# Weights decoded by a sign-carrying Prelu, and all exponentials added ahead of one round of sums

## The chip, the core and the metric

The kernel runs on one core of a Trainium2 chip. The metric is the device time of one execution in microseconds (us). The engines are TensorE (PE, its weight loads PEld), VectorE (DVE), ScalarE (ACT), GpSimd (POOL) and SyncE (SP, which issues every DMA here).

## The reference

Attention with a soft cap, then two feed-forward blocks, all in float32, 2 x 448 tokens, 12 heads of 64:

```python
scores = cap * np.tanh(scale * (q @ k.T) / cap)
attn = np.exp(scores - max); attn = attn / (attn.sum(-1) + 1e-09)
x = attn @ v                                   # 896 tokens x 768
h = x @ w_in                                   # 768 x 2048
g = (a0 + a1*h + a2*h**2 + a3*h**3) / (1 + |b0|*|h| + |b1|*h**2 + 1e-6)
x = g @ w_out                                  # 2048 x 768
h = max(x @ w1, x @ w2, x @ w3)                # three of 768 x 768
out = h @ moe2_w_out                           # 768 x 768
```

The weights come as 64-bit floats. The kernel reads each as two 32-bit words and makes a float32 of them on the chip.

## The kernel before

**Stages.** Heads are worked in six groups d0 to d5 of four heads each (two pairs r). For a group, `scores` (products at L616 and L624) makes seven score tiles; ACT takes tanh of each (L638, or L641 in halves) and then the exponential (L645), once over the three full key tiles of a pair and once over the shared rest of the keys. `weighted_rest` and `weighted` (L669, L688) multiply the exponentials with v. `summed` makes the sums of the exponentials: products with a matrix of ones (L734), four small ones for each tile. Where `ADDED[d]` is 2 (d0 to d2) the three full tiles of a pair are first added on DVE or POOL (`added`, L710), and the products run over that sum and the rest of the keys: 2 rounds. Where it is 0 (d3 to d5) they run over all four: 4 rounds. The sums go through a copy (L745), a DMA out and back, an addition of the guard and a reciprocal (L753, L754), and two more DMAs into a row tile; `scale_pair` multiplies (L776) and splits the result into a high and a low part (L780, L784), the x of the next stage.

Then `up` (L804) multiplies x with w_in in parts of six products, `up` and `rational` make g (L821 to L869), `parts` splits g (L883, L886), `down` multiplies with w_out (L911), `product` with w1 to w3 (L1048) and `output` with the last matrix (L1156). Each product with split operands is three TensorE products.

**Weights.** `decoded` makes a float32 tile of 128 x 768 from a raw tile (768 pairs of words, one DMA of 768 KB). `scale` multiplies the upper words by 2^-112, on ACT (L446) or POOL (L448); `shift` shifts by three and clears the sign (L452, DVE); `rest` puts in three low bits, on DVE (L471) or by a byte copy on ACT (L468); `sign` puts the sign back (L461, DVE). `split` rounds to a high part (L488) and takes the low part (L491).

**What sets the order.** A planner (`Flow`) lays out every operation with a cost, engines that it may run on and due times that follow from TensorE's order; each engine then runs its list in that order, and none overtakes. `SPARE`, `AHEAD`, `NEAR`, `SWITCH` and the costs in `add` are its figures, so a changed cost or operation reorders all engines.

Of the kernel before, what the change touches and what calls it, by code (L numbers as in the profile page):

```python
# [11 lines left out]
U8 = mybir.dt.uint8  # L12
# [16 lines left out]
QGUARD = 1.0 + 1e-6  # L29
CAP = 6  # L30
# [5 lines left out]
WARM = 3  # L36
EARLY = 5

AHEAD, NEAR, LEAVE = 200.0, 30.0, 4
# [7 lines left out]
SPARE = 1.06  # L47
# [11 lines left out]
ADDED = 2, 2, 2, 0, 0, 0  # L59
# [10 lines left out]
class Op:  # L70
    def __init__(self, engines, after, vals, fn, shared, due, leave, ahead, size, mode):
        self.engines, self.after, self.vals, self.fn = engines, after, vals, fn
        self.shared, self.due, self.leave, self.ahead, self.size = shared, due, leave, ahead, size
        self.mode = mode
        self.next, self.soft, self.left, self.ready, self.done, self.on = [], [], 0, 0.0, None, None
# [6 lines left out]
class Flow:  # L82
# [91 lines left out]
    def issue(self):  # L174
# [21 lines left out]
        while left:  # L196
# [4 lines left out]
            while moved:  # L201
                moved = False
                for e in names:
# [5 lines left out]
                    for op in ready:  # L209
# [23 lines left out]
                        if e != first and op.engines[e] > max(0.0, busy[first] - t) + ahead[first] + cost + (not self.scores and e == "act") * BIAS:  # L233
                            ahead[first] += cost
                            continue
# [83 lines left out]
def attention_moe(ctx: ExitStack, tc: tile.TileContext, qk, v, w_in, w_out, w123, w_out2, par, out):  # L319
# [22 lines left out]
    qone = cp.tile([P, 1], F32, name="qone")  # L342
    ones = cp.tile([P, 3, Q], F32, name="ones")
# [50 lines left out]
    con_in = dma(lambda: con, lambda: par.broadcast_to([P, 8]), size=0.004, issue=0.45, due=-20.0)  # L394
# [11 lines left out]
    def first_scalars(e):  # L406
        dve.reciprocal(out=qscale, in_=cap)
        dve.tensor_scalar(out=qscale, in0=qscale, scalar1=D**-0.5, scalar2=None, op0=ALU.mult)
        dve.memset(qone, QGUARD)

    def more_scalars(e):
# [5 lines left out]
    scal = add({"act": 0.8}, more_scalars, [con_in], due=60.0)  # L417
# [3 lines left out]
        [scal], due=60.0,  # L421
# [8 lines left out]
    add({"pe": 3 * WARM * 0.4}, warm_up, [zero], [idle, warm])  # L430
    fl.clock = 4.5
# [7 lines left out]
    def decoded(key, src):  # L439
# [39 lines left out]
        s1 = add({"act": 0.80, "pool": 0.87}, scale, [got], [raw, dec], leave=LEAVE, ahead=AHEAD)  # L479
        s2 = add({"dve": 0.47}, shift, [s1], [dec], shared=True)  # L480
        s3 = add({"dve": 0.87, "act": 1.9}, rest, [s2], [raw, dec], shared=True)
        s4 = add({"dve": 0.87}, sign, [s3], [raw, dec], shared=True)
# [90 lines left out]
    def prep(pi):  # L573
        raw = slot(f"qk{pi}")
        src = qk[divmod(pi, NPAIR)]
        QK[pi] = raw, dma(lambda: two(raw), lambda: src, vals=[raw], size=0.459, issue=0.45, ahead=NEAR)
# [18 lines left out]
    def scores(d, i):  # L595
# [22 lines left out]
        def ends(e):  # L618
# [11 lines left out]
            {"pe": FULL}, products if whole_ else ends, [QK[pi][1] for pi in pis], [QK[pi][0] for pi in pis] + [t],  # L630
# [73 lines left out]
    def added(d, r):  # L704
        y, done = slot(f"es{d}_{r}"), None
        for n in range(ADDED[d]):
# [5 lines left out]
            done = add({"dve": 1.0, "pool": 2.1}, plus, [ex, ez, done], [x, y, z], shared=True)  # L712
        ADDS[d, r] = y, done, lambda: two(y)

    def summed(d):
# [5 lines left out]
        for r in range(2):  # L721
# [3 lines left out]
            rounds.append(es + [E[d, 2 * NFULL]])  # L725
        last = len(rounds[0]) - 1

        def products(e):
            for n in range(last + 1):
                for r in range(2):  # L730
                    x = rounds[r][n][2]()
                    for j in range(2):
                        g = (2 * r + j) * Q
                        pe.matmul(  # L734
                            bank(t)[g : g + Q, :S], ones[:, 0 if n < last else 1 + r], x[:, j], start=n == 0,
# [8 lines left out]
        got = add(  # L744
            {"act": 0.43, "dve": 0.54}, lambda e: copy_on[e](rows[row.at[0]], bank(t)[:, :S]), [dep], [t, row]  # L745
        )
# [5 lines left out]
        def recip(e):  # L752
            dve.tensor_scalar(out=comp[d], in0=comp[d], scalar1=guard, scalar2=None, op0=ALU.add)  # L753
            dve.reciprocal(out=comp[d], in_=comp[d])  # L754

        rc = add({"dve": 0.75}, recip, [back, guard_in])
# [34 lines left out]
    def up(n):  # L791
# [28 lines left out]
        def absolute(e):  # L820
            act.activation(two(a_)[:, i], bank(h)[:, :S], AF.Abs)  # L821
# [4 lines left out]
        def linear(e):  # L826
            if e == "act":
                act.activation(two(t_)[:, i], two(a_)[:, i], AF.Identity, bias=b0, scale=b1)  # L828
            else:
                engine[e].tensor_scalar(  # L830
                    out=two(t_)[:, i], in0=two(a_)[:, i], scalar1=b1, scalar2=b0, op0=ALU.mult, op1=ALU.add
                )
# [398 lines left out]
```

## Time and profile before

| | us |
|---|---|
| median of 3 runs (lowest, highest) | 491.92 (491.77, 492.22) |
| the profiled execution, its own time | 492.5 |
| span of the profiled execution | 490.4 |
| TensorE busy in the span | 482.6 |
| DVE busy | 415.2 |
| ACT busy | 337.2 |
| POOL busy | 91.8 |

The profile has one execution. The span runs from the first to the last instruction; 2.1 us of the execution lie around it. Busy TensorE time counts a product from its issue, so that waits can hide in it. A tile name ends in a number in the order of the instructions and has none in the profile. A line of a timeline is: start, time from the first start to the last end, engine, line, operation, tiles, shape, count, and in brackets the idle time before it with its releaser.

### The profile page before, as it was taken

The numbers are of one execution on the slowest core, as the hardware profiler recorded it, in microseconds if no ns is written. First come the engines' busy times: TensorE is split into PE (matmuls) and PEld (weight loads), VectorE is DVE, ScalarE is ACT, GpSimd is POOL, SyncE is SP. The second block draws the span as 40 slices with busy tenths as digits, with TensorE's granted clock in tenths as the row PEclk, the third lists the DMA queues.
The fourth block names the chain that finished last, engine by engine and source line by source line (L and its number), as shares of the span: only waits on it lengthen the run. The fifth ranks groups of instructions, "written<-read, shape, count | busy, mean of one in ns | idle before, by whom it ended". The sixth has DMA issues, their size and how long they took to land.

```text
span 490.4 us, 6637 instructions
## 1 busy us (share of the span) xinstructions
PE 482.6 (98%) x2508; PEld 399.1 (81%) x2508; DVE 415.2 (85%) x596; ACT 337.2 (69%) x402; POOL 91.8 (19%) x73
## 2 busy tenths in 40 slices
PE   8899999999999999999999999999999999999996
PEld 5233333499899999889999999999999999999996
DVE  0499898989999999999899999889999999999000
ACT  6999998978896889786776756685555345673211
POOL 0313030122121121200000100442443332202000
PEclk9999999999999999999999999999999999999999
DMA  8945535680000321311121576403435030340211
GB/s 301 408 147 204 162 120 183 214 264 6 2 0 1 126 68 64 130 69 60 65 64 65 193 246 212 175 12 130 127 131 190 4 128 2 103 155 0 98 64 65
DMA packets 16448, 58.36 MB, mean 119 GB/s; under 512 B 3592, under 2 KB 6944, under 8 KB 16416
## 3 DMA queue, kind: packets, MB, share of 16 engines
q1 hardware_dynamic: 16416, 57.94, 33.9%
q8 instruction: 19, 0.31, 0.3%
q14 instruction: 13, 0.11, 0.1%
HBM read 55.10 MB, written 2.84 MB: 118 GB/s over the span
## 4 chain that ended last, share of the span: by engine, by line
PE 84%; ACT 6%; DVE 5%; DMA 3%; issue 1%; SPq 0%; DVEq 0%; ACTq 0%
PE b L1048 23%; PE b L911 22%; PE b L804 17%; PE b L1156 9%; PE b L688 4%; PE bb L616 3%; PE b L734 3%; ACT e L638 2%; ACT e L645 2%; PE b L669 1%; DMA rsum<-comp 1%; ACT e L641 1%; DMA row<-rsum 1%; DMA qk<-in_qk_dram 1%; PE b L616 1%
## 5 line engine op out<-in xcount | busy, mean ns | idle before, releaser
L804 PE MATMUL b<-x,whin 128*128 128x448 f32 x384 | 109.8, 368 | 0.3 <-DVE W L838 0.2
L804 PEld LDWEIGHTS b<-x,whin 128*128 128x128 f32 x384 | 71.7, 188 | 9.3 <-issue 2.7
L804 PE MATMUL b<-x,wlin 128*128 128x448 f32 x192 | 70.2, 366 | 0.0
L1048 PE MATMUL b<-T,mh 128*128 128x448 f32 x216 | 61.4, 366 | 0.0
L468 ACT ACTIVATE raw<-raw 128x768 uint8<-128x768 uint8 x31 | 60.1, 1984 | 0.1
L1048 PEld LDWEIGHTS b<-T,mh 128*128 128x128 f32 x216 | 40.6, 188 | 3.1
L1048 PE MATMUL b<-T,ml 128*128 128x448 f32 x108 | 39.5, 366 | 0.0
L804 PEld LDWEIGHTS b<-x,wlin 128*128 128x128 f32 x192 | 36.1, 188 | 2.8
L645 ACT ACTIVATE e<-e,con 128x2688 f32<-128x2688 f32 (+1 forms) x18 | 37.5, 2120 | 0.1
L911 PE MATMUL b<-gl,whoa 128*128 128x448 f32 x96 | 35.2, 367 | 0.2 <-DVE gl L886 0.2
L911 PE MATMUL b<-gh,wlob 128*128 128x448 f32 x96 | 35.2, 367 | 0.0
L911 PE MATMUL b<-gh,wloa 128*128 128x448 f32 x96 | 35.1, 366 | 0.0
L911 PE MATMUL b<-gh,whob 128*128 128x448 f32 x96 | 35.1, 366 | 0.0
L911 PE MATMUL b<-gh,whoa 128*128 128x448 f32 x96 | 35.1, 366 | 0.0
L911 PE MATMUL b<-gl,whob 128*128 128x448 f32 x96 | 35.1, 366 | 0.0
L638 ACT ACTIVATE e<-bb,qscale 128x896 f32<-128x896 f32 x31 | 31.4, 1069 | 3.4 <-PE bb L616 3.0
L1048 PE MATMUL b<-B,mh 128*128 128x448 f32 x108 | 30.7, 366 | 0.0
L688 PE MATMUL b<-e,v 128*64 128x448 f32 x144 | 28.8, 545 | 1.5 <-ACT e L645 1.4
L843 POOL TENSOR_TENSOR T<-T,A 128x448 f32<-128x448 f32 x10 | 13.4, 1340 | 81.0 <-ACT T L828 67.3
L1156 PE MATMUL b<-who,h3h 128*128 128x384 f32 x84 | 28.1, 335 | 0.0
L1156 PE MATMUL b<-who,h3l 128*128 128x384 f32 x84 | 28.1, 335 | 0.0
L1156 PE MATMUL b<-wlo,h3h 128*128 128x384 f32 x84 | 28.1, 335 | 0.0
(161 smaller groups left out, 1126.7 us busy)
## 6 DMA issues: line engine op xcount, KB each, us to landing
raw<-in_w_out_dram SPq DMA_DIRECT2D x22, 768.0 KB, 4.5
raw<-in_w_dram SPq DMA_DIRECT2D x18, 768.0 KB, 4.3
raw<-in_w_in_dram SPq DMA_DIRECT2D x16, 768.0 KB, 5.6
qk<-in_qk_dram SPq DMA_DIRECT2D x12, 448.0 KB, 6.0
v<-in_v_dram SPq DMA_DIRECT2D x6, 448.0 KB, 9.9
row<-rsum SPq DMA_DIRECT2D x24, 112.0 KB, 2.8
out_dram<-ob SPq DMA_DIRECT2D x6, 384.0 KB, 2.8
out_dram<-ob SPq DMA_DIRECT2D x2, 192.0 KB, 1.9
```

What stands on the lines that cost most here:

```text
L468: act.activation(byte[:, 4::8], byte[:, 3::8], AF.Copy, scale=1 / 32, bias=-31 / 64)
L616: pe.matmul(pair(t, j)[:, :S], k[rr], q[rr], start=True, stop=True)
L638: act.activation(view(), twins[t.at[0] // 2][:, :, :S], AF.Tanh, scale=qscale)
L641: act.activation(view()[:, j], pair(t, j)[:, :S], AF.Tanh, scale=qscale)
L645: act.activation(all_, all_, AF.Exp, scale=cap)
L688: pe.matmul(bank(o)[j * D : j * D + D, :S], whole(vr, n, r, j), view()[:, j], start=False, stop=n == NFULL - 1,)
L734: pe.matmul(bank(t)[g : g + Q, :S], ones[:, 0 if n < last else 1 + r], x[:, j], start=n == 0, stop=n == last, tile_position=(0, g),)
L804: pe.matmul(bank(h)[:, :S], w_, x_, start=cc == 0 and i == 0, stop=cc == NCC - 1 and i == len(terms) - 1)
L843: engine[e].tensor_tensor(out=two(t_)[:, i], in0=two(t_)[:, i], in1=two(a_)[:, i], op=ALU.mult)
L911: pe.matmul(bank(a)[:, :S], w_, g_, start=count[half, o, b] == 1, stop=count[half, o, b] == 3 * NFC)
L1048: pe.matmul(bank(o)[:, :S], w_, m_, start=cc == 0 and i == 0, stop=cc == 2 and i == 2)
L1156: pe.matmul(bank(o)[:, :NH], h_, w_, start=ocs[0] == 0 and i == 0, stop=ocs[-1] == NCC - 1 and i == len(terms) - 1,)
```

## The change

**Sums.** `ADDED` becomes 3 for all six groups: the three full tiles of a pair are added and then, on half of the partitions, the rest of the keys; one round of products with ones is left for each group. The guard is added in the copy out of the bank (a bias), and the reciprocal stands alone.

**Weights.** On ACT the scaling is a Prelu whose factor for negative words brings the sign through a later shift. The low bits are made in the raw tile, on ACT (a copy from unsigned 32-bit words) or on DVE (shift and mask), and `join` shifts and merges in one DVE operation. Where the scaling ran on POOL, `join` has a second DVE operation that puts the sign in. Of the 56 weights the new order scales 33 on ACT and 23 on POOL (before 39 and 17), and makes the low bits on ACT in 46 and on DVE in 10 (before 31 and 25).

**The quotient's denominator.** |b0||h| comes from an Abs with a scale, |b1|h^2 from a Square with the root of |b1| (made once by a few tiny operations), and DVE or POOL adds them; the linear term of L828 and L830 goes.

**Start.** The first q,k tile is loaded in two pieces, the constants' DMA stands behind three loads, and seven in place of nine warm-up products run. The planner's `NEAR`, `SPARE` and a few due times differ.

```diff
-ADDED = 2, 2, 2, 0, 0, 0
+ADDED = 3, 3, 3, 3, 3, 3
...
-    con_in = dma(lambda: con, lambda: par.broadcast_to([P, 8]), size=0.004, issue=0.45, due=-20.0)
+    con_in = dma(lambda: con, lambda: par.broadcast_to([P, 8]), size=0.004, issue=0.45, due=2.0)
...
-        for _ in range(3 * WARM):
+        for _ in range(WARM):
...
         def scale(e):
-            o, i = flat(dec), f32(raws[raw.at[0]][:, :, 1])
+            x = f32(raws[raw.at[0]][:, :, 1])
             if e == "act":
-                act.activation(o, i, AF.Copy, scale=2.0**-112)
-            else:
-                engine[e].tensor_scalar(out=o, in0=i, scalar1=2.0**-112, scalar2=0.0, op0=ALU.mult, op1=ALU.add)
-
-        def shift(e):
-            t = flat(dec).bitcast(I32)
-            dve.tensor_scalar(
-                out=t, in0=t, scalar1=3, scalar2=0x7FFFFFF8, op0=ALU.logical_shift_left, op1=ALU.bitwise_and
-            )
-
-
-
-        def sign(e):
-            t = flat(dec).bitcast(I32)
-            mask = -0x80000000 if s3.on == "dve" else -0x7FFFFFF9
-            dve.scalar_tensor_tensor(
-                out=t, in0=raws[raw.at[0]][:, :, 1], scalar=mask, in1=t, op0=ALU.bitwise_and, op1=ALU.bitwise_or
-            )
-
-        def rest(e):
+                act.activation(flat(dec), x, AF.Prelu, scale=2.0**-112, alpha=-(2.0**32))
+                return
+            s4.engines["dve"] = (JOIN + SIGN) * SPARE
+            engine[e].tensor_scalar(out=flat(dec), in0=x, scalar1=2.0**-112, scalar2=0.0, op0=ALU.mult, op1=ALU.add)
+
+        def bits(e):
+            o = raws[raw.at[0]][:, :, 0]
             if e == "act":
-                byte = raws[raw.at[0]].bitcast(U8).rearrange("p n t -> p (n t)")
-                act.activation(byte[:, 4::8], byte[:, 3::8], AF.Copy, scale=1 / 32, bias=-31 / 64)
+                act.activation(o, raws[raw.at[0]].bitcast(U32)[:, :, 0], AF.Copy, scale=LOW / 2.0**32)
                 return
+            dve.tensor_scalar(out=o, in0=o, scalar1=29, scalar2=7, op0=ALU.logical_shift_right, op1=ALU.bitwise_and)
+
+        def join(e):
             t = flat(dec).bitcast(I32)
             dve.scalar_tensor_tensor(
-                out=t, in0=raws[raw.at[0]][:, :, 0], scalar=29, in1=t, op0=ALU.logical_shift_right, op1=ALU.bitwise_or
+                out=t, in0=t, scalar=3, in1=raws[raw.at[0]][:, :, 0], op0=ALU.logical_shift_left, op1=ALU.bitwise_or
             )
+            if s1.on != "act":
+                dve.scalar_tensor_tensor(
+                    out=t, in0=raws[raw.at[0]][:, :, 1], scalar=-0x80000000, in1=t, op0=ALU.bitwise_and,
+                    op1=ALU.bitwise_or,
+                )
...
+        if pi:
+            got = dma(lambda: two(raw), lambda: src, vals=[raw], size=0.459, issue=0.45, ahead=NEAR)
+            QK[pi] = raw, got, got
+            return
+        src, cut = src.rearrange("p a s -> p (a s)"), S + P
+        near = dma(lambda: flat(raw, cut), lambda: src[:, :cut], vals=[raw], size=0.295, issue=0.45, due=0.0)
+        far = dma(lambda: flat(raw, 2 * S)[:, cut:], lambda: src[:, cut:], vals=[raw], size=0.164, issue=0.45, ahead=NEAR)
...
+        if ADDED[d] == NFULL:
+            x, ex, one = E[d, 2 * NFULL]
+            rr = slice(r * D, r * D + D)
+
+            def ends(e):
+                engine[e].tensor_tensor(out=two(y)[rr], in0=two(y)[rr], in1=one()[rr], op=ALU.add)
+
+            done = add({"dve": 1.0, "pool": 2.1}, ends, [ex, done], [x, y], shared=True)
...
-            rounds.append(es + [E[d, 2 * NFULL]])
+            rounds.append(es if ADDED[d] == NFULL else es + [E[d, 2 * NFULL]])
...
+                act.activation(rows[row.at[0]], bank(t)[:, :S], AF.Identity, bias=guard)
...
-            act.activation(two(a_)[:, i], bank(h)[:, :S], AF.Abs)
+            act.activation(two(a_)[:, i], bank(h)[:, :S], AF.Abs, scale=b0)
...
+        def square(e):
+            act.activation(two(t_)[:, i], bank(h)[:, :S], AF.Square, scale=root)
...
-            engine[e].tensor_tensor(out=two(t_)[:, i], in0=two(t_)[:, i], in1=two(a_)[:, i], op=ALU.mult)
+            engine[e].tensor_tensor(out=two(t_)[:, i], in0=two(t_)[:, i], in1=two(a_)[:, i], op=ALU.add)
```

On TensorE at the sums of d3, before: its products with v, two score products, and the first products with ones over the three tiles of each pair (`e_0`, `e_1`); the last two rows stand there twice more, and then four over the rest (`e_6_417`).

```order
L688 MATMUL b_82<-e_0_471,v_346 64x448 x6
L688 MATMUL b_81<-e_1_513,v_346 64x448 x6
L616 MATMUL bb_91<-qk_323 128x448 x2
L616 MATMUL bb_92<-qk_323 128x448 x2
L734 MATMUL b_82<-e_0_471,ones 32x448 x2
L734 MATMUL b_82<-e_1_513,ones 32x448 x2
```

The same place after:

```order
L629 MATMUL bb_94<-qk_383 128x448 x2
L755 MATMUL b_615<-es_0_470,ones 32x448 x2
L755 MATMUL b_615<-es_1_513,ones 32x448 x2
L825 MATMUL b_616<-x_0_497,whin_460 128x448 x2
L825 MATMUL b_616<-x_0_497,wlin_523 128x448
L825 MATMUL b_616<-x_1_506,whin_460 128x448 x2
L825 MATMUL b_616<-x_1_506,wlin_523 128x448
L825 MATMUL b_615<-x_0_497,whin_578 128x448 x2
```

One round over the sums that DVE makes (`es_0`, `es_1`) is left, and two parts of L825 (line 804 before) follow; the second of them, over `whin_578`, goes to the bank that the sums have just been in (`b_615`).

On TensorE at the end of attention, before: the last products of d5's sums (`e_0_581`, `e_1_645` for the third time, `e_6_523`), its products with v, and the next part of L804.

```order
L734 MATMUL b_715<-e_0_581,ones 32x448 x2
L734 MATMUL b_715<-e_1_645,ones 32x448 x2
L734 MATMUL b_715<-e_6_523,ones 32x448 x4
L688 MATMUL b_84<-e_0_581,v_435 64x448 x6
L688 MATMUL b_81<-e_1_645,v_435 64x448 x6
L804 MATMUL b_714<-x_2_528,whin_464 128x448 x2
```

The same place after (d4's products with v, d5's rest, a part of L825, d5's sums, and d5's products with v):

```order
L701 MATMUL b_85<-e_0_468,v_403 64x448 x6
L701 MATMUL b_613<-e_1_511,v_403 64x448 x6
L682 MATMUL b_614<-e_6_551,v_484 64x448 x2
L682 MATMUL b_84<-e_6_551,v_484 64x448 x2
L825 MATMUL b_86<-x_4_622,whin_372 128x448 x2
L825 MATMUL b_86<-x_4_622,wlin_385 128x448
L825 MATMUL b_86<-x_5_630,whin_372 128x448 x2
L825 MATMUL b_86<-x_5_630,wlin_385 128x448
L755 MATMUL b_85<-es_0_645,ones 32x448 x2
L755 MATMUL b_85<-es_1_674,ones 32x448 x2
L701 MATMUL b_614<-e_0_561,v_484 64x448 x6
L701 MATMUL b_84<-e_1_601,v_484 64x448 x6
```

The sums of d5 now come from `es_0_645` and `es_1_674`, which DVE makes, and still stand ahead of the products with v.

On DVE in the same stretch, before: decoding, x of d2 and the reciprocal of d3.

```order
L776 TENSOR_TENSOR xu_423<-xu_423,row_78 128x448
L699 COPY xu_629<-b_82 128x448
L776 TENSOR_TENSOR xu_423<-xu_423,row_77 128x448
L753 TENSOR_SCALAR comp_108<-comp_108,guard 128x14
L754 RECIPROCAL comp_108<-comp_108 128x14
L784 TENSOR_TENSOR x_5_638<-xu_423,x_5_638 128x448
L461 SCALAR_TENSOR_TENSOR decoa_584<-raw_76,decoa_584 128x768
L452 TENSOR_SCALAR decin_667<-decin_667 128x768
L471 SCALAR_TENSOR_TENSOR decin_667<-raw_74,decin_667 128x768
```

After, from the copy of d3's sums (`row_81<-b_615`) on:

```order
L769 TENSOR_SCALAR row_81<-b_615,guard 128x448
L712 COPY xu_634<-b_85 128x448
L805 TENSOR_TENSOR x_5_630<-xu_438,x_5_630 128x448
L723 TENSOR_TENSOR es_0_645<-e_0_561 128x896
L494 CAST whin_654<-decin_326 128x768
L723 TENSOR_TENSOR es_0_645<-es_0_645,e_0_561 128x896
L769 TENSOR_SCALAR row_82<-b_614,guard 128x448
L712 COPY xu_634<-b_84 128x448
L723 TENSOR_TENSOR es_1_674<-e_1_601 128x896
L731 TENSOR_TENSOR es_0_645<-es_0_645,e_6_551 64x896
L723 TENSOR_TENSOR es_1_674<-es_1_674,e_1_601 128x896
```

The adds of d5 stand between that copy and the next reciprocals; the decoding that stood here has moved behind them.

## Rows read from the trace of the kernel before

**Rows 1.** Windows: start:end, length, then busy us (instructions) of PE, PEld, DVE, ACT, POOL, clock, DMA share, GB/s.

```profile
60.00:95.50 35.50, 35.50 (x231) 14.46 (x232) 32.17 (x53) 32.71 (x35) 6.32 (x4) 1.00 0.53 185
95.50:124.00 28.50, 28.34 (x140) 24.55 (x137) 25.51 (x36) 23.73 (x32) 7.24 (x6) 1.00 0.37 116
124.00:198.00 74.00, 74.00 (x366) 68.53 (x367) 72.58 (x93) 61.44 (x80) 12.22 (x7) 1.00 0.15 48
```

**Rows 2.** The chain that ended last, in order of time: start, us, what.

```profile
1.18 3.88 DMA qk<-in_qk_dram
...
6.18 1.90 ACT e L638 x2
...
9.13 1.79 ACT e L638 x2
10.93 1.05 ACT e L641 x2
...
13.77 0.93 ACT e L645
...
15.75 2.42 ACT e L645
...
80.86 3.14 PE b L734 x32
...
86.39 0.91 PE b L669 x8
...
148.22 7.30 PE b L804 x36
```

**Rows 3.** Timeline of PE around the end of attention.

```profile
93.01 4.73 PE L688 MATMUL b<-e,v 128*64 128x448 f32 x24
97.67 0.67 PE L804 MATMUL b<-x,whin 128*128 128x448 f32 x2
```

**Rows 4.** Timeline of DVE from its first add to d1's x.

```profile
18.20 1.09 DVE L710 TENSOR_TENSOR es<-e 128x896 f32<-128x896 f32 x1 [14.07 <-ACT e L645]
20.10 0.56 DVE L452 TENSOR_SCALAR decin<-decin 128x768 int32<-128x768 int32 x1 [0.80 <-POOL decin L448]
20.57 1.90 DVE L710 TENSOR_TENSOR es<-es,e 128x896 f32<-128x896 f32 x1
...
24.56 1.08 DVE L710 TENSOR_TENSOR es<-e 128x896 f32<-128x896 f32 x1
25.56 0.95 DVE L461 SCALAR_TENSOR_TENSOR decin<-raw,decin 128x768 int32<-128x768 int32 x1
26.43 1.08 DVE L710 TENSOR_TENSOR es<-es,e 128x896 f32<-128x896 f32 x1
27.43 0.61 DVE L699 COPY xu<-b 128x448 f32<-128x448 f32 x1
27.96 1.01 DVE L452 TENSOR_SCALAR decin<-decin 128x768 int32<-128x768 int32 x2
28.90 1.82 DVE L471 SCALAR_TENSOR_TENSOR decin<-raw,decin 128x768 int32<-128x768 int32 x2
...
52.59 0.62 DVE L699 COPY xu<-b 128x448 f32<-128x448 f32 x1 [1.39 <-PE b L688]
...
61.28 0.67 DVE L776 TENSOR_TENSOR xu<-xu,row 128x448 f32<-128x448 f32 x1
```

**Rows 5.** Timeline of POOL, its first two decodes.

```profile
18.36 1.70 POOL L448 TENSOR_SCALAR decin<-raw 128x768 f32<-128x768 f32 x1 [13.68 <-DMA raw<-in_w_in_dram]
20.26 1.26 POOL L448 TENSOR_SCALAR decin<-raw 128x768 f32<-128x768 f32 x1 [0.20 <-DMA raw<-in_w_in_dram]
```

**Rows 6.** Groups by line and shape: count, busy us, mean ns, idle before.

```profile
L468 ACT ACTIVATE raw<-raw 128x768 uint8<-128x768 uint8 x31 | 60.1, 1984 | 0.1
...
L446 ACT ACTIVATE decm<-raw 128x768 f32<-128x768 f32 x14 | 12.7, 914 | 7.8 <-DMA raw<-in_w_dram 5.8 <-PE b L1048 1.9
```

**Rows 7.** Timeline of SP, the first four loads of q and k.

```profile
1.18 1.84 SPq L391 DMA_DIRECT2D qk<-in_qk_dram  x4
```

More of the change, by code (lines that the diff above doesn't have):

```diff
@@ L57 @@
 STAGGER = 4
[L59 removed]
+FIRST = 2
+ADDED = 3, 3, 3, 3, 3, 3
 class Val:
@@ L232, in issue @@
                             continue
-                        if e != first and op.engines[e] > max(0.0, busy[first] - t) + ahead[first] + cost + (not self.scores and e == "act") * BIAS:
+                        if e != first and op.engines[e] + op.dear.get(e, 0.0) > max(0.0, busy[first] - t) + ahead[first] + cost + (not self.scores and e == "act") * BIAS:
                             ahead[first] += cost
@@ L342, in attention_moe @@
     qone = cp.tile([P, 1], F32, name="qone")
+    root = cp.tile([P, 1], F32, name="root")
+    half = cp.tile([P, 1], F32, name="half")
+    tiny = cp.tile([P, 1], F32, name="tiny")
     ones = cp.tile([P, 3, Q], F32, name="ones")
@@ L426, in warm_up @@
         z = two(idle)[:, 0]
-        for _ in range(3 * WARM):
+        for _ in range(WARM):
             pe.matmul(bank(warm)[:, :S], z[:, :P], z, start=True, stop=True)
-    add({"pe": 3 * WARM * 0.4}, warm_up, [zero], [idle, warm])
-    fl.clock = 4.5
+    add({"pe": WARM * 0.4}, warm_up, [zero], [idle, warm])
+    fl.clock = 3.8
     class Weight:
@@ L478, in decoded @@
         )
[L479 to L482, printed above, removed]
+        s1 = add({"act": 0.83, "pool": 0.87, "dve": 0.47}, scale, [got], [raw, dec], leave=LEAVE, ahead=AHEAD)
+        s1.dear = {"pool": DEAR[0], "dve": DEAR[1]}
+        s2 = add({"act": 0.83, "dve": 0.47}, bits, [got], [raw], shared=True, leave=LEAVE, ahead=AHEAD)
+        s2.dear = {"dve": DEAR[2]}
+        s4 = add({"dve": JOIN}, join, [s1, s2], [raw, dec], shared=True)
         return dec, s4
@@ L575, in prep @@
         src = qk[divmod(pi, NPAIR)]
-        QK[pi] = raw, dma(lambda: two(raw), lambda: src, vals=[raw], size=0.459, issue=0.45, ahead=NEAR)
+        if pi:
[5 more added lines that the diff above has]
+        far = dma(lambda: flat(raw, 2 * S)[:, cut:], lambda: src[:, cut:], vals=[raw], size=0.164, issue=0.45, ahead=NEAR)
+        QK[pi] = raw, near, far
     def values(d):
@@ L734, in products @@
                         pe.matmul(
-                            bank(t)[g : g + Q, :S], ones[:, 0 if n < last else 1 + r], x[:, j], start=n == 0,
+                            bank(t)[g : g + Q, :S], ones[:, 1 + r if n == last and ADDED[d] < NFULL else 0], x[:, j], start=n == 0,
                             stop=n == last, tile_position=(0, g),
@@ L743, in summed, with guarded @@
         )
[L744 to L746 removed]
+        def guarded(e):
+            if e == "act":
+                act.activation(rows[row.at[0]], bank(t)[:, :S], AF.Identity, bias=guard)
+            else:
+                dve.tensor_scalar(out=rows[row.at[0]], in0=bank(t)[:, :S], scalar1=guard, scalar2=None, op0=ALU.add)
+        got = add({"act": 0.55, "dve": 0.60}, guarded, [dep, guard_in], [t, row])
         last_copy.append(got)
@@ L750, in summed @@
         back = dma(lambda: comp[d], lambda: flat_, [out_], size=0.007, issue=0.4)
[L752 to L756, printed above, removed]
+        rc = add({"dve": 0.35}, lambda e: dve.reciprocal(out=comp[d], in_=comp[d]), [back])
         dst = rsum[d].rearrange("r j s -> (r j s)").rearrange("(p k) -> p k", p=P)
@@ L862, in newton @@
         def newton(e):
-            dve.scalar_tensor_tensor(out=two(t_), in0=two(t_), scalar=qone, in1=two(a_), op0=ALU.add, op1=ALU.mult)
+            dve.scalar_tensor_tensor(out=two(t_), in0=two(t_), scalar=QGUARD, in1=two(a_), op0=ALU.add, op1=ALU.mult)
         def numer(e):
@@ L998, in attention_moe, with guess, heron @@
     table = add({"act": 1.3}, lambda e: act.preload_act_table_set("natural_log_exp_and_others"), last_tanh)
+    def guess(e):
+        act.activation(root, b1, AF.Ln, bias=tiny)
+        act.activation(root, root, AF.Exp, scale=0.5)
+    def heron(e):
+        dve.reciprocal(out=half, in_=root)
+        dve.scalar_tensor_tensor(out=half, in0=half, scalar=b1, in1=root, op0=ALU.mult, op1=ALU.add)
+        dve.tensor_scalar(out=root, in0=half, scalar1=0.5, scalar2=None, op0=ALU.mult)
+    rooted = add({"dve": 0.6}, heron, [add({"act": 0.45}, guess, [table, scal])])
     early = 0
```

39 lines of the change are left out of this document (19 added, 20 removed).

## The prediction

> **What bounds the kernel now.** I read the windows by stage first. From 60 us on TensorE is busy through every window, 28.34 of 28.50 us where attention hands over to the feed-forward block [rows 1]. Busy time can hide waits, so the chain of waits comes second. From 6.18 to about 30 us it lies on ACT, which does tanh and exponentials without a gap; from there to the end nearly all of it is TensorE work that follows TensorE work [rows 2]. So whatever takes products out of TensorE's list shortens the kernel, as long as its partners deliver in time. Among these DVE is the next: 32.17 of 35.50 us in the second half of attention and 72.58 of 74.00 us after it, ACT 32.71 and 61.44 [rows 1]. POOL is nearly idle.
>
> The profiled execution took 492.5 us, 490.4 of them span; the median of the runs is 491.92, 0.6 less. I make the sum on the span and take the difference off the median.
>
> **The sums on TensorE.** A program product with ones is two in the trace. Before: 16 of these for each of d0 to d2, 32 for each of d3 to d5, 144. After: 8 for each group, 48. The 96 that go cost 3.14 us for 32, 0.098 each [rows 2], so 9.4 us leave TensorE's list. To compare, I take the end of the last product with v: 97.67 in the trace [rows 3]. The old order has four six-product parts of L804 ahead of it, the new order seven of L825; a part is 7.30/6 = 1.22 us [rows 2]. Before, the same work would have ended at 97.67 + 3 x 1.22 = 101.3. Without a wait the new one ends at 91.9.
>
> **What ACT allows.** 31 tanh of 896 columns at 0.895, 22 halves at 0.525, 12 long exponentials at 2.42 and 6 short ones at 0.93 [rows 2] make 27.7 + 11.6 + 29.0 + 5.6 = 73.9 us; two copies of sums and one weight cast, at most a tanh of their size each (0.53 and 0.9), make 75.8. From 6.18 the last exponential ends at 82.0 or a little later.
>
> **What DVE must do.** This is the term that decides. Start-to-start prices in a stretch without waits: an add of 896 columns 1.00, a 768-column operation with two sources 0.87, one with a single source 0.47, a 448-column copy 0.53 [rows 4]. For an operation on half of the partitions I take the full 1.00, since its columns are the same; the bound below is 0.5, by its elements. How such a sum stands to the clock is read from before: from the first add (18.20) to d1's x (61.28) DVE had 12 adds, 15 two-source and 10 single-source operations, 14 of 448 columns and two pairs of tiny ones (0.8): 38.0 us. The clock moved 43.1, of which 0.80 and 1.39 were waits [rows 4]. So work takes 40.9/38.0 = 1.077 of its price.
>
> In the new order, from the first add to the copy of d3's sums (`row_81<-b_615`) stand 20 full and 10 half adds, 10 two-source and 7 single-source operations, 24 of 448 columns and three reciprocals: 30 + 8.7 + 3.3 + 12.7 + 0.6 = 55.3, on the clock 59.6. The first add follows three decoded weights; the third raw tile now ends after 5.6 MB of loads, where before the first ended after 5.8 MB and POOL took it up at 18.36 [rows 5]. With POOL's 1.3 and two joins of 0.87 that is 20.9. The copy ends at 20.9 + 59.6 = 80.5.
>
> **Where TensorE meets it.** The second part of L825 after d3's sums writes the bank that this copy reads, so TensorE waits for it. From the copy on it has two parts, two rests (0.91), two rounds with ones (0.78) and two groups of products with v (4.66) [rows 2, 3]: 15.1 us; by its own work alone it would begin these at 91.9 - 15.1 = 76.8. Before the last round it also needs d5's last add, which comes after 9.5 us of DVE prices, 10.2 on the clock: 90.7. TensorE is there at 80.5 + 9.7 = 90.2. It waits half a microsecond, and the last product with v ends at 90.7 + 0.8 + 4.7 = 96.1. The exponentials (82.0) are ready by then. Gain: 101.3 - 96.1 = 5.2 us; of the 9.4 taken out, 4.2 are given back to waiting on DVE.
>
> **After attention.** TensorE is full there before and after. Each weight needs fewer operations: shift (0.47) and sign (0.87) go where ACT scales, and the low bits on ACT no longer go byte by byte. A byte copy takes 1984 ns, the 4-byte operation with the same spacing 914 [rows 6]; the new one moves 4-byte words, so I price it at 914 and keep 1984 as its other end. The Prelu replaces a copy of the same form and gets the same 914; bounds from the same two rows. The Trainium skill (ScalarE: Activation LUTs, What ACT_TABLE_LOAD costs) says that an ACTIVATE takes one element a cycle whatever its function, about 186 ns + 0.833 ns an element; for 768 elements my estimate from it is 826 ns. By that rule the byte copy should have cost the same, and the trace has more than twice that, so the rule alone doesn't settle the new form. The low bits on DVE, single-source on spaced words, cost 0.47 or at most 0.87 as a two-source operation; three stand between the adds, +1.2 at worst, in the range. Abs gains a scale, Square takes the place of the linear step: one operation each for one; nothing on the path. Relief of DVE and ACT here is worth at most the 0.16 us that TensorE lacked [rows 1]; I count nothing.
>
> **The start.** First scores can come up to 0.7 us sooner: the first load is no longer behind the constants (one issue, 0.46 [rows 7]) and a third shorter. But the constants are now fourth, issued some 1.4 us later, and tanh needs them. Q and k took 3.88 us from issue to landing [rows 2]; by that the constants land at 6.0 and tanh starts about 6.5, later by 0.3. Bounds -0.4 to +0.5; I take 0. Two weight loads move ahead of q and k of d2, which TensorE wants only after d0's products with v. The warm-up's two products lie in the wait for the first load.
>
> **Rivals.**
>
> A, full cover: DVE keeps up (half adds at 0.5 alone give 5 x 1.08 = 5.4 us back up to the copy), ACT is done at 82.0, and all 9.4 us show: 482.5. For it: POOL is nearly idle. Against it: no add went to POOL, and prices of before needed 1.077.
>
> B, DVE is later than reckoned: waits like before's 2.2 us in the same stretch, plus 1.2 for spaced words: the copy at 83.9, the end at 99.5, gain 1.8: 490.1. DVE's add at 20.57 took 1.90 us while POOL decoded from 20.26 [rows 4, 5]. Such meetings are in the 1.077, with about as many POOL decodes in the stretch; more adds can meet more of them, which is this rival again. The Trainium skill (SBUF — State Buffer, Who interferes with whom) says that a VectorE operation with two SBUF inputs and a GpSimd operation that reads SBUF exclude each other for the whole instruction; those two rows agree with it, and it speaks against an exchange of TensorE products for DVE adds beside POOL.
>
> C, slower: ACT's low bits cost what the byte copy did. Then 46 of them take 1.98, where there were 31, and the planner set them at under 0.9. Three stand between the table load and the first W of the feed-forward block, so g is late by 3 us at the first product with w_out; after that ACT has 74.0 - 61.4 = 12.6 us of room in 124 to 198 [rows 1], which some twelve such operations eat, and each weight's low part comes about 1 us late to an order laid out for less. With 8 us lost in all, three at first and some five over that stretch, the 5.2 turn into about 3 us of loss: 495. It decides from about 1.6 us an operation.
>
> That the change doesn't do what it says is excluded for the products: the order has 48. Whether DVE makes up for it is B.
>
> **How the numbers follow.** Forecast: 491.9 - 5.2 = 486.7, chance 0.52, itself 484.5 to 488.8. A 0.22, B 0.16, C 0.10. The range holds 8 in 10 if it takes in A's and most of B's: 482.0 to 490.5. A measurement tells about 0.2%, 1 us. Forecast and A are faster beyond that; of B three quarters are; so faster 0.86, same 0.04, slower 0.10.
>
> **What would show it.** 48 products with ones in TensorE's rows; the last product with v ending at 95 to 97 with seven parts ahead; waits of TensorE in attention's last fifth that end on DVE, at the part after d3's sums and at d5's sums; ACT's last exponential by 83 to 84; low bits on ACT at 0.9 us, not 2. If TensorE waits on ACT in mid-attention, or for x of the second batch after it, or if the gain lies after 124 us, the reasoning is wrong.

## The result, and the profile after

The changed kernel is slower by 1%: 497.01 us median (496.0 to 498.67) against 491.86 for the kernel before beside it, ratio 1.0107, 95% interval 1.0079 to 1.0135. The forecast was 486.7. The profiled execution of after took 496.0 us, 494.2 of them span (before 492.5 and 490.4), so by spans the forecast missed 9.0 us.

The same three windows as [rows 1], of after (columns as there):

```profile
60.00:95.50 35.50, 34.79 (x194) 15.49 (x188) 35.24 (x51) 34.25 (x36) 2.01 (x2) 1.00 0.15 43
95.50:124.00 28.50, 27.46 (x134) 22.16 (x130) 27.23 (x39) 20.75 (x34) 7.75 (x6) 1.00 0.33 105
124.00:198.00 74.00, 72.56 (x354) 65.80 (x354) 70.65 (x85) 59.55 (x84) 19.65 (x13) 1.00 0.26 86
```

TensorE lacked 0.2 us in all in [rows 1]; now it lacks 0.7, 1.0 and 1.4 us, and DVE is busy almost without a gap in the second half of attention (35.24 of 35.50). The chain that ended last, by engine (page of after, part 4):

```profile
PE 59%; DVE 22%; ACT 12%; issue 3%; DMA 2%; SPq 1%; POOL 0%; DVEq 0%
```

Before, 84% of that chain was TensorE's and 5% DVE's. ACT's timeline of after at the start:

```profile
9.10 0.20 ACT L423 ACTIVATE absb<-con 128x2 f32<-128x2 f32 x1 [7.09 <-DMA con<-in_par_dram]
...
9.55 1.91 ACT L651 ACTIVATE e<-bb,qscale 128x896 f32<-128x896 f32 x2
```

Tanh starts at 9.55, not at 6.18 as in [rows 2], and what it waited for is the load of the constants. DVE's timeline of after: the first add, the copy of d3's sums, the last add of d5.

```profile
23.95 1.08 DVE L723 TENSOR_TENSOR es<-e 128x896 f32<-128x896 f32 x1
...
82.88 0.68 DVE L769 TENSOR_SCALAR row<-b,guard 128x448 f32<-128x448 f32 x1
...
92.82 1.09 DVE L731 TENSOR_TENSOR es<-es,e 64x896 f32<-64x896 f32 x1
```

TensorE's timeline of after: a wait at the start, d5's one round with ones, the last products with v [rows 3], the first product of the third stage.

```profile
10.61 3.08 PE L637 MATMUL bb<-qk 64*64 64x448 f32 x16 [2.69 <-ACT e L651]
...
93.83 1.08 PE L755 MATMUL b<-es,ones 128*32 128x448 f32 x8
94.84 4.73 PE L701 MATMUL b<-e,v 128*64 128x448 f32 x24
...
332.06 0.57 PE L1075 MATMUL b<-B,mh 128*128 128x448 f32 x2
```

The last product with v ends at 99.57, seven parts of L825 ahead of it. The prediction's equal-work end of before is 101.3, so 1.7 us were won by then. But the third stage begins at 332.06, in before at 327.83: 6 us were lost in the first feed-forward block. (Products follow each other 0.203 us apart there. Where the distance is longer, the excess adds up to 6.6 us from 100 us to the third stage; before, to 1.3. These are called waits by starts below.) TensorE's waits from 100 us on (total us, times, longest):

```profile
PE b L927 <- DVE gl L902: 2.4, 2, 1.4
PE b L825 <- DVE W L854: 1.1, 1, 1.1
PE b L825 <- DVE x L805: 0.3, 1, 0.3
```

And one of them in the timelines of ACT, DVE and PE:

```profile
171.54 0.63 ACT L848 ACTIVATE T<-b,root 128x448 f32<-128x448 f32 x1
...
172.21 0.68 DVE L854 SCALAR_TENSOR_TENSOR W<-W,con,b 128x448 f32<-128x448 f32 x1 [1.00 <-ACT T L848]
...
172.94 0.67 PE L825 MATMUL b<-x,whin 128*128 128x448 f32 x2 [1.11 <-DVE W L854]
```

DVE's second product reads W and the bank of h. It doesn't read T, yet it waits for the Square that writes T. What the two share is the bank, which both only read. So I read these rows as turns: the readers of a bank on two engines run one after the other, in the order of the code. The Square made a fifth reader, where the linear step had read A in SBUF. The read itself did not get slower: DVE's second product takes 676 ns, 674 before. This turn can be seen in before too; its DVE waits after 100 us begin with a product that doesn't read A:

```profile
DVE W L835 <- ACT A L821: 3.0, 6, 0.9
```

The Trainium skill (PSUM — Partial Sum Buffer, PSUM bank collisions raise a hardware error) says that two engines on one bank must be kept apart, a read by ScalarE and one by VectorE included. The rows agree that the program does so; whether the chip needs it was not tried.

### The profile page after: what moved, and what is told of

The parts are those of the page before. It is cut to its first block, busy times and chain, and to the rows that moved or that the text cites. A ratio compares the mean times of both kernels' runs of the same rounds, so it can differ in the third digit from the quotient of the medians.

```text
span 494.2 us, 6389 instructions
## 1 busy us (share of the span) xinstructions
PE 478.9 (97%) x2410; PEld 394.4 (80%) x2410; DVE 416.1 (84%) x561; ACT 317.9 (64%) x426; POOL 86.9 (18%) x75
## 4 chain that ended last, share of the span: by engine, by line
PE 59%; DVE 22%; ACT 12%; issue 3%; DMA 2%; SPq 1%; POOL 0%; DVEq 0%
PE b L1075 23%; PE b L927 15%; PE b L1183 9%; PE b L825 6%; DVE W L854 2%; PE b L701 2%; DVE T L879 2%; DVE W L851 2%; DMA raw<-in_w_in_dram 2%; ACT A L842 2%; ACT T L848 2%; DVE decin L471 2%; PE bb L629 2%; DVE W L885 2%; DVE gl L902 2%
## 5 line engine op out<-in xcount | busy, mean ns | idle before, releaser
L825 PE MATMUL b<-x,whin 128*128 128x448 f32 x384 | 111.0, 370 | 1.7 <-DVE W L854 1.1
L825 PEld LDWEIGHTS b<-x,whin 128*128 128x128 f32 x384 | 70.9, 188 | 14.1 <-issue 3.4
L825 PE MATMUL b<-x,wlin 128*128 128x448 f32 x192 | 70.3, 366 | 0.0
L465 ACT ACTIVATE raw<-raw 128x768 int32<-128x768 uint32 x46 | 42.0, 918 | 19.2 <-DMA raw<-in_w_dram 9.9
L825 PEld LDWEIGHTS b<-x,wlin 128*128 128x128 f32 x192 | 36.1, 188 | 3.0
L859 POOL TENSOR_TENSOR T<-T,A 128x448 f32<-128x448 f32 x17 | 24.2, 1423 | 73.8 <-ACT T L848 73.8
L1198 ACT COPY ob<-b 128x384 f32<-128x384 f32 x13 | 6.3, 482 | 36.2 <-PE b L1183 36.2
```

The source lines that it names most:

```text
L465: act.activation(o, raws[raw.at[0]].bitcast(U32)[:, :, 0], AF.Copy, scale=LOW / 2.0**32)
L825: pe.matmul(bank(h)[:, :S], w_, x_, start=cc == 0 and i == 0, stop=cc == NCC - 1 and i == len(terms) - 1)
L859: engine[e].tensor_tensor(out=two(t_)[:, i], in0=two(t_)[:, i], in1=two(a_)[:, i], op=ALU.add)
```

## The experiments

Ratios are to the kernel before, run beside each. Letters in the expectations stand for theories: S that the late constants cost time, K that the turns at the bank do, R that all waits come from the late start, D that the new decoding and sums load DVE too much, G that the entry to the feed-forward block (the first g) sets the time whatever attention saves, L that any new order with the constants first is as good, M that a planner that knows the turns does it without the change.

| run | median us | ratio, 95% interval |
|---|---|---|
| e1 constants first | 495.31 | 1.0046, 1.0009 to 1.0084 |
| e2 denominator from SBUF | 493.29 | 1.0017, 0.9990 to 1.0044 |
| e3 both | 492.07 | 0.9983, 0.9952 to 1.0013 |
| e4 before, linear from bank | 497.17 | 1.0085, 1.0057 to 1.0113 |
| e5 before, sums alone | 507.73 | 1.0311, 1.0268 to 1.0354 |
| e6 before, decoding alone | 499.41 | 1.0152, 1.0094 to 1.0210 |
| e7 change less two | 498.52 | 1.0126, 1.0075 to 1.0177 |
| e8 change less three | 494.25 | 1.0048, 1.0019 to 1.0076 |
| e9 before, one round | 489.29 | 0.9943, 0.9915 to 0.9972 |
| e10 rule, Square | 488.49 | 0.9926, 0.9900 to 0.9951 |
| e11 rule, linear, six numbers | 496.14 | 1.0068, 1.0038 to 1.0099 |
| e12 both, no half adds | 489.65 | 0.9946, 0.9928 to 0.9963 |
| e13 constants first, no rule | 493.04 | 1.0009, 0.9988 to 1.0031 |
| e14 rule, constants late | 500.57 | 1.0169, 1.0130 to 1.0207 |
| e15 e10's order, linear | 487.60 | 0.9890, 0.9860 to 0.9921 |
| e16 e10's order, constants late | 491.07 | 0.9956, 0.9937 to 0.9976 |
| e17 before, rule | 492.75 | 1.0010, 0.9977 to 1.0043 |
| e18 change less two, rule | 491.20 | 0.9978, 0.9944 to 1.0012 |

The planner lays out all engines anew when a cost or a dependence changes. So the runs that settle a cause keep the order word for word and change one step or one DMA; the others say so.

### One DMA or one operand, order kept

e1:

```diff
-    con_in = dma(lambda: con, lambda: par.broadcast_to([P, 8]), size=0.004, issue=0.45, due=2.0)
+    nc.sync.dma_start(out=con, in_=par.broadcast_to([P, 8]))
+    con_in = add({"sp": 0.45}, lambda e: None, size=0.004, due=2.0)
```

> The changed kernel with one DMA moved: the constants are issued first, as before the change, ahead of the first load of q and k. The order on every other engine stays word for word. Theory S (the late constants cost what tanh started late, 9.55 against 6.18 us, 3.4 us): first tanh at about 6, last product with v ends at 96.1 instead of 99.5, the kernel takes 497.0 - 3.4 = 493.6 if the waits of TensorE after attention (5.2 us) are of another cause. Rival R (those waits come from the same delay: the order after attention was laid out for partners 3.4 us earlier): the waits go as well, 488 to 489. If the constants cost nothing, 497.

```profile
6.92 1.01 ACT L652 ACTIVATE e<-bb,qscale 128x896 f32<-128x896 f32 x1 [2.38 <-PE bb L630]
```

That is e1's first tanh (ACT's timeline; its lines are one higher). The last product with v ends at 97.92, 1.65 us sooner, and the kernel is 1.7 us faster by medians, 3.0 by the two ratios. So S holds in kind, at half to all of its price. The waits after 100 us stay (2.6 us on gl, 1.1 on W), so R falls.

e2:

```diff
-            act.activation(two(t_)[:, i], bank(h)[:, :S], AF.Square, scale=root)
+            act.activation(two(t_)[:, i], two(a_)[:, i], AF.Identity, bias=b0, scale=b1)
```

(and Abs without scale, and the product in place of the sum, as before)

> The changed kernel with the old denominator in the new order: Abs without a scale, and in the Square's place the linear step, which reads A in SBUF and not the bank of h; POOL or DVE multiplies where it added. Theory K (the Square is a fifth reader of the bank, and readers of one bank take turns in program order, so DVE's second product waits for ACT and TensorE for both): of the 5.2 us of waits after 99.5 us at least 4 go, the kernel takes 492 to 493, although the step from SBUF is slower by itself (761 against 636 ns). Rival R (the waits are the late start's): 497 within 1. Rival D (the new decoding or the added sums load DVE too much): 497 within 1.

TensorE's waits of e2 from 100 us on:

```profile
PE b L927 <- DVE gl L902: 1.7, 2, 1.4
PE b L825 <- DVE W L854: 0.8, 1, 0.8
```

The waits fall by 1.3 us here, and short ones that the view doesn't name fall as well: the sum by starts goes from 6.6 to 4.0, the third stage begins 2.9 us sooner, and the kernel gains 3.7 by medians, 4.4 by the ratios. The step from SBUF takes 762 ns, the Square took 636: ACT does more and the kernel is faster. K is right in kind; of the 4 us of waits that it wanted gone at least, 2.6 go by starts.

e3 is e1 and e2 together.

> Both edits together: constants first and the denominator from SBUF, in the new order. Theories S and K add up: 497.0 - 3.4 - 4.5 = 489. If R is right, this equals the first of the two (488 to 489). If both are wrong, 495 or more.

The two add up to 4.9 us by medians (6.1 by ratios) and lead back to the time of before, not below it to the 489 expected. The last product with v ends at 98.25, 3 us ahead of equal work in before; the third stage begins at 327.92, where before has 327.83. The 3 us go into waits on gl (1.6) and W (1.0) and into small ones.

e4 puts the suspected cost into the kernel before:

```diff
-                act.activation(two(t_)[:, i], two(a_)[:, i], AF.Identity, bias=b0, scale=b1)
+                act.activation(two(t_)[:, i], bank(h)[:, :S], AF.Identity, bias=b0, scale=b1)
```

(the same operand on DVE)

> The kernel before in its own order, with one operand changed: the linear step of the denominator reads the bank of h in place of A in SBUF (|h| is left out there, so g is another number). ACT's step gets cheaper by itself (761 to about 640 ns). Theory K: the linear step joins the readers that take turns at the bank, so TensorE gets waits between 95 and 330 us that the kernel before hasn't, 3 to 6 us: 495 to 498. Rivals R and D: 491.9 within 1, or a little less.

Waits of e4 from 95 us on, all engines:

```profile
ACT T L828 <- DVE W L835: 5.6, 7, 1.5
...
DVE W L838 <- ACT T L828: 3.7, 6, 1.2
...
PE b L804 <- ACT T L828: 1.6, 2, 1.0
PE b L804 <- DVE W L838: 1.4, 2, 0.8
```

One operand costs 5.1 us by medians, 4.2 by ratio, and makes the waits of after in the old order (5.5 us of them by starts, for 1.3). ACT's step by itself took 724 ns from the bank, 761 from SBUF, so it is not the step that got dearer. Part of the trace's loss is not K's: q and k came 1.5 us later in the profiled execution (tanh at 7.63), the slowest of the ten.

### Parts by themselves, laid out anew

e5 and e6 put the new sums, or the new decoding, into the kernel before; e7 takes the late constants and the Square out of the change and plans with that; e8 takes the sums out too. One line of each:

```diff
e5
-ADDED = 2, 2, 2, 0, 0, 0
+ADDED = 3, 3, 3, 3, 3, 3
e6
-                act.activation(o, i, AF.Copy, scale=2.0**-112)
+                act.activation(flat(dec), x, AF.Prelu, scale=2.0**-112, alpha=-(2.0**32))
e7
-        sq = add({"act": 0.5}, square, [dep, rooted], [h, t_])
+        li = add({"act": 0.66, "dve": 0.42}, linear, [ab], [a_, t_])
e8, beside e7's
-ADDED = 3, 3, 3, 3, 3, 3
+ADDED = 2, 2, 2, 0, 0, 0
```

> The kernel before with one part of the change: all exponentials added on DVE or POOL ahead of one round of ones (48 products in place of 144). The planner lays all engines out anew. Forecast's step (96 products and 9.4 us off TensorE, some 5 us of it kept): 486 to 488. Theory G (at the entry to the feed-forward block the first g is bound by DVE and ACT, so what TensorE saves in attention it waits for there, and old decoding costs DVE more per weight): last product with v 3 to 5 us ahead of an equal amount of work in the kernel before, but the third stage begins within 1.5 us of 327.8, and the kernel takes 491 to 494.

> The kernel before with one part of the change: the new decoding of weights (Prelu, low bits on ACT at 0.92 us in place of 1.98, one DVE join in place of shift, low bits and sign). The planner lays all engines out anew. If the decoding is nothing on the path (forecast): 491 to 493. If its relief of DVE counts at the entry to the feed-forward block: 489 to 491. If the low bits on ACT delay g (rival C of the prediction): 494 to 496.

> The changed kernel without the two parts found to cost time (constants first again, denominator by Abs and the linear step, on ACT or DVE), and this time planned with their costs, so the order is another than in the run of both edits, with 168 products of w_in ahead of the first product with w_out (138 there, 150 in the kernel before). Theory G: the waits at the first g shrink since more work stands ahead of it; 488 to 491. If the order laid out for the wrong costs was all that held it back: 486 to 487. If the sums and the decoding are worth nothing: 492.

> As the run before, with the old sums too (2, 2, 2, 0, 0, 0 adds), so that the new decoding, the shorter first load and the planner's numbers are what is left of the change. Against the run with the new sums it tells what the sums are worth beside the new decoding. Forecast's step: the sums give 4 to 5 us, so this one is slower by that. Theory G: within 1.5 us of it. By itself: 489 to 493.

All four missed every expectation for their time, on the slow side. By equal work (parts of w_in and products with ones counted) the last product with v is 3.5 us ahead of before in e5 and 2.8 in e7, which have the new sums, and 0.6 and 2.1 us behind in e6 and e8, which have the old. All four start the third stage later than before, by 2.4 (e8) to 13.5 us (e5). TensorE's largest waits of e5:

```profile
PE b L813 <- ACT A L830: 3.6, 2, 3.3
PE b L920 <- DVE gl L895: 2.6, 3, 1.1
PE b L920 <- ACT gh L892: 2.0, 1, 2.0
```

TensorE's waits that the view names after 100 us add up to 11.8 us in e5, 5.2 in e6, 6.6 in e7 and 1.0 in e8, for 0.4 in before, so these runs price orders, not parts. e7 against e3 shows it: much the same work, 6.4 us apart.

### What the sums are worth

e9 takes the rounds out of before and gives DVE nothing; e12 takes 12 adds from e3. Orders kept.

```diff
-            for n in range(last + 1):
+            for n in (last,):
```

> The kernel before in its own order, word for word on every engine, with the first of the two rounds of ones for d0 to d2 and the first three of four for d3 to d5 left out (that part of the sums is left out there): the 96 traced products go, and DVE gets nothing in exchange. It is the most that the removal alone can bring in that order. Forecast's premise (TensorE's own list sets the time from 60 us on): most of the 9.4 us show, 483 to 485. Theory G (ACT's exponentials, DVE's queue and the first g set the entry to the feed-forward block; TensorE waits for what it saves): last product with v near 93, third stage no earlier than 325, 489 to 491.

```diff
-                engine[e].tensor_tensor(out=two(y)[rr], in0=two(y)[rr], in1=one()[rr], op=ALU.add)
+                pass
```

> The run with both edits (constants first, denominator from SBUF), same order, with the 12 adds on half of the partitions left out (the last 64 keys are left out of the sums there): 12.8 us less for DVE in attention, nothing else. If DVE sets the end of attention (forecast, rival B): last product with v 2 to 4 us before 98.25, and the first g and the third stage follow by as much, 488 to 490. If ACT's exponentials set it: last product with v at 97 to 98, 491.5 to 492.5.

TensorE's timeline of e9:

```profile
86.33 4.73 PE L688 MATMUL b<-e,v 128*64 128x448 f32 x24
```

It stands 6.7 us earlier than in [rows 3]. The third stage begins at 323.06, 4.8 earlier; the profiled execution took 487.47 and is the fastest of the ten, the median gains 2.8. So of 9.4 us taken from TensorE at most 6.7 show even where nobody else does their work. The median is where G had it, but both places in the trace come sooner than G allows, and the forecast's premise (7 to 9 us) was too high. In e12 the last product with v ends at 95.65 and the third stage begins 2.3 us sooner than in e3: 13.0 us of DVE work in attention cost 2.4 us.

### A planner that knows the turns

The rule: ACT or DVE doesn't start on a bank of h while the other reads it.

```diff
+                        if e in ("act", "dve") and any(
+                            self.turn.get(i, (e, 0.0))[0] != e and self.turn[i][1] > t + 1e-9
+                            for v in op.vals if v.kind in TURN and v.at for i in v.at
+                        ):
+                            continue
```

(`turn` holds, per bank of h, its last reader's engine and end.) e10 has it in the change with `due=-20.0` for the constants again, e13 has that `due` alone, e17 the rule in the kernel before.

> The changed kernel, Square from the bank included, with constants first and one rule added to the planner: ACT and DVE don't read one bank of h at the same time, so a reader is placed behind the reader of the other engine. Engines are laid out anew. Theory K (turns at the bank that the planner didn't know of made the order wrong): waits of TensorE on W and T go, 489 to 492. If the turns cost time whatever the order: 494 to 496.

> The changed kernel with constants first in the planner's list and without the rule on the bank's turns; the engines are laid out anew, the Square reads the bank. Beside the run with the rule (488.5) it tells what the rule is worth. Theory K (the order has to know the turns): waits of TensorE on W, T or gl between 95 and 330 us as in the changed kernel, 492 to 496. Rival L (any new order with constants first would have done it): 488 to 490.

> The kernel before with nothing but the rule on the bank's turns in its planner; laid out anew. It tells whether the 488 us of the changed kernel with the rule come from the change or from the rule alone. Theory K with the change worth some 4 us: 491 to 494, since the order of the kernel before has next to no waits to lose (0.4 us of TensorE's after 100 us). Rival M (the rule does it all): 487 to 489.

Windows of e10, columns as above:

```profile
60.00:95.50 35.50, 33.65 (x180) 14.83 (x178) 35.16 (x51) 33.55 (x36) 3.54 (x2) 1.00 0.20 63
95.50:124.00 28.50, 28.50 (x145) 24.93 (x142) 27.20 (x37) 23.37 (x37) 9.49 (x8) 1.00 0.41 133
124.00:198.00 74.00, 74.00 (x365) 68.02 (x364) 73.21 (x89) 63.11 (x89) 18.27 (x12) 1.00 0.29 97
```

TensorE is full from 95.5 us on, with the Square still reading the bank, and the third stage begins at 324.59. The change with its constants first and this rule beats both kernels. Without the rule (e13) the median is 4.5 us higher, with waits on W, gl and T again (in a profiled execution that was the slowest of twelve, 497.29); with the rule alone (e17) the kernel before stays where it was. So neither a new order with the constants first nor the rule alone brings the gain, and the change can be worth it. That the turns are what the rule cured is argued, not shown: e10 and e13 differ in their whole order. G falls: the entry to the feed-forward block can take what attention saves.

e14 is e10 with the change's `due=2.0`, e18 is e7 with the rule, and e11 is e18 with other numbers in the planner (SPARE, too, which its expectation leaves out):

```diff
-AHEAD, NEAR, LEAVE = 200.0, 20.0, 4
+AHEAD, NEAR, LEAVE = 200.0, 20.0, 3
-LATE, KEEP = 40.0, 4
+LATE, KEEP = 30.0, 3
-SPARE = 1.05
+SPARE = 1.06
-SHARE = 0.5
+SHARE = 0.3
-FIRST = 2
+FIRST = 1
```

> The changed kernel with the rule on the bank's turns and the constants fourth in the planner's list as in the change; laid out anew. Theory K with S: no waits on W or T after attention, tanh late as in the changed kernel, so 488.5 + 1.7 to 3.4 = 490 to 492. Rival L: 495 or more.

> The rule on the bank's turns with constants first and the denominator by Abs and the linear step from SBUF, and five numbers of the planner chosen anew (slots kept back 3 and 3, due 30 us ahead, 0.3 of POOL's time for the port, one token tile in two parts). If the sums and the decoding are worth what the forecast gave them once the two costs are gone and the order knows the turns: 486 to 489, faster than both kernels. Theory G: 490 to 492.

> The change less its two dear parts (constants first, linear step from SBUF), planned as in the run of 498.5 us, and with the rule on the bank's turns. If the rule is what a new layout lacks: 488 to 491. If a layout is good or bad for other reasons (waits on g that the planner doesn't foresee): 492 to 498.

TensorE's waits of e14 from 100 us on:

```profile
PE b L942 <- DVE gl L917: 3.1, 3, 1.8
PE b L840 <- ACT T L863: 1.4, 1, 1.4
PE b L942 <- ACT gh L914: 0.7, 1, 0.7
```

The rule is no cure for every order. e18 is 7.3 us below e7, its twin without the rule; but e14 is 3.6 us above its own twin, the changed kernel, and e14 and e11, both with the rule, are slower than before and wait for g (gh, gl) above all. e14 came out where rival L had it, not K; e11 missed all that was expected. What makes the planner promise g too early there stays open; no run isolates it. A long wait cost e14 more than itself: behind the one of 1.8 us, which ends at 268.59, the granted clock is 0.66 from 268 to 273 us, and products start 0.37 us apart until 271.7 (1.2 GHz), 0.21 before (2.4 GHz).

### In the good order

e15 is e10 with e2's operands, e16 is e10 with the constants' DMA issued behind three loads of q and k.

> The run with the rule (488.5) in its own order, word for word, with Abs without a scale and the linear step from SBUF in the Square's place, as in the earlier run of the denominator. Theory K: in an order that knows the turns the fifth reader costs nothing that shows, so 488 to 490 (the step from SBUF is 0.1 us slower by itself). If reading the bank costs time whatever the order: 485 to 487.

> The run with the rule (488.5) in its own order on every other engine, with the constants issued fourth, behind three loads of q and k, as in the change. Theory S prices the start alone in an order without later waits: tanh later by 2.6 to 3.7 us, the kernel by 1.7 (as the moved load gave back in the changed order) to 3.4: 490.2 to 491.9.

e15 is the fastest of all, 487.60, between the two ranges expected. It gains 0.9 on e10 by medians, 1.8 by ratios, with intervals that overlap: in this order, which knows the turns, the fifth reader costs 2 us at most, or nothing. In e16 tanh starts at 9.69 and the kernel is 2.6 us slower by medians, 1.5 by ratios, with no wait of TensorE after 100 us: the late constants by themselves. Its profiled execution has one wait more in attention, 1.78 us for a tanh up to 81.24, and a granted clock of 0.66 from 80 to 85 us behind it.

## Why the prediction was wrong

**Two steps failed, and a premise.** "After attention ... Square takes the place of the linear step: one operation each for one; nothing on the path": by count and by ACT's time it is one for one (636 and 634 ns against 761 and 538), but the operand moved from SBUF to the bank, and the turns there cost 2.9 us by the trace of e2, 3.7 to 4.4 by its time. And "The start ... I take 0", with bounds of -0.4 to +0.5: the constants landed at 9.1, not at 6.0, and tanh came 3.4 us late. The 6.0 took over the landing time of q and k as before's first large load, though three loads stand ahead of the constants now. Price: 1.5 to 3.0 us (e1, e16). The premise is "TensorE is full there before and after", which was read from before alone: the forecast treated the new order as if it had no waits of its own. With both costs taken out (e3) this order still loses 3 us between the last product with v and the third stage.

**The sum, mended.** 3.5 us late at the last product with v (99.57 for 96.1), 6.0 between it and the third stage, 0.5 back after that: the 9.0 us by which the spans miss. Of the 6.0 the turns of the Square are 2.5 by the trace of e2, more by its time; what makes the 3 that stay in e3 is open. It is not in the work itself, since e10, with the same work in another order, has no such waits.

**The sums** were right in kind. 48 products with ones stand in the order. DVE's term held: 59.6 us were reckoned from the first add to the end of the copy of d3's sums, and 59.6 passed (23.95 to 83.56). A half add takes the full price (1080 ns; 1079 on all partitions):

```profile
L731 DVE TENSOR_TENSOR es<-es,e 64x896 f32<-64x896 f32 x12 | 13.0, 1080 | 0.2
```

Its start was wrong: first add at 23.95 for 20.9. Some 1.4 us of that are the late constants (22.55 in e1). In the rest the third raw tile was late: POOL took it up at 19.03 in e1, where the forecast's sum had 17.9 (20.9 less 1.3 and two joins); and then the low bits beside POOL (1.31) and two joins at 0.96 took 3.5 us for 3.0. d5's last add ended at 93.9 for 90.7, and the round with ones began at 93.83, at once. The waits on DVE that the forecast looked for at the part after d3's sums and at d5's round came to 0.2 us in all, because TensorE was late itself. The gain of 5.2 was 2.7 to 3.4 us by equal work at the end of attention where the constants come first (e1, e3, e7, e10), and in e10 it reaches the end of the kernel.

**ACT**: 75.8 us from the first tanh to the last exponential were 78.05 (9.55 to 87.60); TensorE waited for it 0.7 us in mid-attention, and 1.5 for a copy that DVE made late (L712, at 42.1).

**Rivals.** A didn't come. B's DVE was late, by its start and not by its prices: that B's copy at 83.9, end at 99.5 and gain of 1.8 are nearly the 83.6, 99.6 and 1.7 measured is luck. C had the sign and nearly the time, by a mechanism that wasn't there: the low bits cost what the forecast took.

```profile
L465 ACT ACTIVATE raw<-raw 128x768 int32<-128x768 uint32 x46 | 42.0, 918 | 19.2 <-DMA raw<-in_w_dram 9.9 <-DMA raw<-in_w_out_dram 9.2
```

Missing was the rival that before's own waits named: DVE's product that waits for Abs, whose result it doesn't read.

## What to carry to other kernels

A wait for an instruction whose result the waiter doesn't read names a shared resource; here it is the bank. Count an operation by what its operands lie in, not only by its time. Telling the planner of the turns gained 4.5 and 7.3 us in two pairs of orders, nothing in a third, and lost 3.6 in a fourth, so look at the waits of each order that it lays out. To price one part of a change under a planner, keep the order and change one operand: parts laid out anew differed by up to 16 us from before, for reasons of their orders that no run isolates.

## What was not expected of the hardware

The 4 KB of constants landed some 3 us after their issue as the first load, and 7.0 us after it (2.11 to 9.1) as the fourth. While they were under way the transfers behind them slowed down too. Windows of after, then of before (the last two columns are DMA share and GB/s):

```profile
4.00:6.00 2.00, 2.00 (x7) 0.91 (x8) 0.00 (x0) 0.00 (x0) 0.00 (x0) 1.00 0.70 121
```

```profile
4.00:6.00 2.00, 1.89 (x9) 0.98 (x10) 0.13 (x2) 0.27 (x2) 0.21 (x1) 1.00 1.04 409
```

So the first weight came late as well: DVE took it up at 14.33, in e1 at 12.93. Which of the loads slowed which was not isolated.

After TensorE's 2.69 us of waiting at the start its granted clock was 0.66 from 10 to 15 us, so part of that stretch ran at 1.2 GHz, and 16 products of L637 took 3.08 us, which took 1.93 in before at full clock. Such a wait doesn't always bring it: e2 waits 2.91 us at the same place and shows a granted clock of 1.00 from 10 to 15 us.
